# Retention and gated network on one core: idle matmuls, turn order and the third pair's place

## The chip, the core and the metric

The kernel runs on one core of a Trainium2 chip. The metric is the device time of one execution in microseconds. A core has five engines that run their own instruction streams and meet through semaphores: TensorE (PE: matrix products, with weight loads listed as PEld), VectorE (DVE), ScalarE (ACT), GpSimd (POOL) and SyncE (SP, which here issues the DMAs). All times below are microseconds unless another unit is given.

## The reference

```python
def _attn_ref(q, k, v):                      # (8 batches, 8 heads, 576, 64)
    scores = scale * np.matmul(q, k.transpose(0, 1, 3, 2))
    gamma = 1.0 - 2.0 ** (-5.0 - np.arange(H))
    Dmat = np.where(rel >= 0, gamma[:, None, None] ** rel[None, :, :], 0.0)
    return np.matmul(scores * Dmat[None, :, :, :], v)

def _moe_ref(x, w_gate, w_val, w_out):       # x: 4608 x 512; 512 x 1536, 1536 x 512
    gate = 1.0 / (1.0 + np.exp(-(x @ w_gate)))
    return gate * (x @ w_val) @ w_out
```

The heads' outputs of the first function, put side by side, are the rows `x` of the second. There is no softmax; the decay is a power of a number per head, so it can be put into q and k row by row, and what earlier rows contribute can be carried in a state of 64 x 64 per head.

## The kernel before, in words

**Two ways through attention.** Each batch has 576 rows: four chunks of 128 and a short one of 64. Six chunks (batch 0, chunks 0 to 3, and batch 1, chunks 0 and 1) are taken as three *pairs* of 256 rows (`PAIRS`), the other 34 chunks as *steps* (`STEPS`). Every chunk ends as columns of `xT`, the input of the gated network, transposed. 768 columns come from the pairs, the rest follow step by step.

**A pair.** `load_pair` asks for k, q, k, q, v, v (two tiles each, g = 0 and 1, four heads in a tile). `cast_pair` multiplies k (POOL) and q (DVE) by the decay table and narrows v (POOL). `turn` calls `pair_t` (L301): four PE transposes into a PSUM bank and a copy by ACT (L316). `pair_qk` (L318) makes 16 small score products into two banks, and DVE multiplies both by the triangle (L330). `pair_intra` (L356) multiplies these by v, `pair_st` (L333) adds k times v to the state bank, `tile_sv` (L346) copies the state to SBUF in two halves on the engines that it is given (L351), `pair_inter` (L370) adds state times q, and `pair_out` (L378) copies the result to `xT` (L380).

**Idle matmuls.** `fill(n)` (L149) takes a PSUM bank of the `ffn` pool (three banks, shared with the turns of the first two pairs) and runs n products of zeros, 128 rows by 512 columns, whose result nobody reads.

**A step.** `casts_to(s)` (L447) issues for each step up to s: the loads of a following step, POOL's casts of k (L247) and q (L257), the DMA transpose of both (`cross`, L284, on SP), and POOL's cast of v (L268). Then come phases: `phase_qk` (scores, L390, and the mask on DVE, L392), `phase_pv` (L409, L411, and ACT's copy to `xT`, L413) and, in all but short chunks, two `phase_st` (L423, state, with DVE's copies, L429). `order` (L433) lists the phases; `run_phase` (L457) puts `casts_to(s + 3)` ahead of each score phase and ACT's dense copy of the next step's v (`cast_dense`, L278) behind scores and outputs. Buffers for the cast k, q and v go round in fours.

**The order of everything.** The schedule is manual: every engine runs its instructions in the order in which the program lists them. The head is a straight list (L614 to L762): pairs one and two; the gated network's first 512 columns (`h_both`, L592: sigmoid products hg and value products hv for 12 column groups); then the first output products (`op_first`, L720, 12 groups for each of four row blocks) with the third pair between them. After it the loop over `BLOCKS` (L766) runs the network on blocks of 256, 384 and 512 columns, in units of eight products (`h_units`, `op_units`), and between units `advance` runs as many phases as have come due, in proportion to the columns done. `store` copies an output to SBUF, and `tick` issues its DMA on SP some units later. SP thus carries, in one queue and in program order, loads, transposes and stores.

The functions that the diff touches and their callers are printed here with the line numbers of the profile.

Of the kernel before, what the change touches and what calls it, by code (L numbers as in the profile page):

```python
# [9 lines left out]
FP32 = mybir.dt.float32  # L10
# [6 lines left out]
def kernel(  # L17
# [19 lines left out]
    nc = tc.nc  # L37
# [4 lines left out]
    P = 128  # L42
    M = H // 2
    NC = (S + P - 1) // P
# [12 lines left out]
    tr_psum = ctx.enter_context(tc.tile_pool(name="tr_psum", bufs=1, space=PS))  # L57
# [85 lines left out]
    LEAD_CAST = 3  # L143
# [5 lines left out]
    def fill(n):  # L149

        ps = ffn_psum.tile([P, 512], FP32, tag="ffn", name=f"idle_{fill.at}")
        fill.at += 1
        for i in range(n):
            nc.tensor.matmul(ps, lhsT=blank[:, 0:P], rhs=blank, start=True, stop=True)  # L154

    fill.at = 0
    fill(12)
    def tables(shape, pattern, step, put):

        pos = consts.tile([P, pattern[0][1], pattern[1][1]], FP32, name=f"pos{step}")  # L160
# [60 lines left out]
    xT = consts.tile([P, M, NT], BF16)  # L221
# [5 lines left out]
    def cast_pair(nm, A, g, eng):  # L227

        if (nm, A) not in natural:
            natural[nm, A] = osb_pool.tile([P, 2, H, D], BF16, tag="osb", name=f"{nm}p_{A}")  # L230
        o = natural[nm, A][:, :, g * M:(g + 1) * M, :].rearrange("p r h d -> p h r d")
        i = parts.pop((nm, "pair", A, g))
        if nm == "v":
            eng(out=o, in_=i)
        else:
            tab = (ktab2 if nm == "k" else qtab2)[:, PAIRS[A][1], g * M:(g + 1) * M, :].unsqueeze(3).to_broadcast([P, M, 2, D])
            eng.tensor_tensor(out=o, in0=i, in1=tab, op=ALU.mult)
# [33 lines left out]
    def cast_dense(s, j):  # L271

        if s >= NS or STEPS[s][1] == NC - 1:
            return
        if j == 0:
            natural["vs", s] = nat_pool.tile([P, 2, M, D], BF16, tag="vs", name=f"vs_{s}", bufs=2)
        for hh in range(2):
            nc.scalar.copy(out=natural["vs", s][half(hh), j], in_=loaded[s][0][half(j), hh::2, :])  # L278
# [36 lines left out]
            o = turned["qp", A][:, 2 * g:2 * g + 2, :].rearrange("p m (t r) -> p m r t", r=2)  # L315
        eng(out=o, in_=ps)  # L316

    def pair_qk(A, g, psum, tag):  # L318
        ps = [psum.tile([P, 2, 2, P], FP32, tag=tag, name=f"qkp_{A}_{g}_{hh}") for hh in range(2)]
        for i in range(2):  # L320
            m = 2 * g + i
            for r in range(2):
                for a in range(2):
                    for hh in range(2):
                        nc.tensor.matmul(ps[hh][half(a), i, r, :], lhsT=turned["kp", A][half(hh), m, r, half(a)],  # L325
                                         rhs=turned["qp", A][half(hh), m, a * P:(a + 1) * P], start=True, stop=True)
        if g == 0:
            probs["p", A] = att_pool.tile([P, 2, M, 2, P], BF16, tag="ptp", name=f"ptp_{A}", bufs=1)
        for hh in range(2):
            nc.vector.tensor_tensor(out=probs["p", A][:, hh, 2 * g:2 * g + 2], in0=ps[hh],  # L330
                                    in1=trip.unsqueeze(1).to_broadcast([P, 2, 2, P]), op=ALU.mult)
# [14 lines left out]
    def tile_sv(A, a, engs):  # L346
        b, a2 = PAIRS[A]
        c = 2 * a2 + a
        sb = sbd[4 if (b, c) == (0, 3) else (2 * A + a) % 4]
        for hh in range(2):  # L350
            engs[hh](out=sb[half(hh), :, half(hh)], in_=st_tiles[b][half(hh)])  # L351
        state[b, c, 1] = sb
# [3 lines left out]
    def pair_intra(A, g, a):  # L356
        s = 2 * A + a
        if g == 0:
            pair_ps[s] = (tr_psum if a else pv_psum).tile([P, M, P], FP32, tag="tr" if a else "pv", name=f"pvp_{s}")
        ps = pair_ps[s]  # L360
        for i in range(2):
            m = 2 * g + i
            for r in range(2):
                for hh in range(2):
                    nc.tensor.matmul(ps[half(hh), m, :], lhsT=natural["v", A][half(a), r, 2 * m + hh, :],
                                     rhs=probs["p", A][half(a), hh, m, r, :],
                                     start=(m == 0 and r == 0), stop=(m == M - 1 and r == 1),
                                     skip_group_check=True)

    def pair_inter(A, a):  # L370
        b, a2 = PAIRS[A]
        c = 2 * a2 + a
        for m in range(M):
            nc.tensor.matmul(pair_ps[2 * A + a][:, m, :], lhsT=state[b, c - 1, 1][:, m, :],
                             rhs=turned["qp", A][:, m, a * P:(a + 1) * P],
                             start=False, stop=(m == M - 1), skip_group_check=True)

    def pair_out(A, a, eng):  # L378
        t0 = (2 * A + a) * P
        eng(out=xT[:, :, t0:t0 + P], in_=pair_ps[2 * A + a])  # L380

    def phase_qk(s):
        n = width[STEPS[s][1]]
# [50 lines left out]
    for s in range(NS):  # L434
        if STEPS[s][1] < NC - 1:
            order += [("st0", s), ("qk", s), ("st1", s), ("pv", s)]
        else:
            order += [("qk", s), ("pv", s)]

    done = {"ld": 0, "cast": 0}  # L440

# [5 lines left out]
    def casts_to(s):  # L447
        while done["cast"] <= min(NS - 1, s):
            x = done["cast"]
            loads_to(x + (1 if x < 12 else 2))  # L450
            cast_k(x)
            cast_q(x)
            cross(x)
            cast_v(x)
            done["cast"] += 1

    def run_phase(kind, s):  # L457
        if kind == "qk":
            casts_to(s + LEAD_CAST)
            phase_qk(s)  # L460
            cast_dense(s + 1, 0)
        elif kind == "pv":
            phase_pv(s)
            cast_dense(s + 1, 1)
        else:
            phase_st(s, int(kind[2]))
# [52 lines left out]
    def store(opp, r0, hold, eng=None):  # L519

        ob = osb_pool.tile([P, DM], FP32, tag="osb", name=f"ob_{r0}")
        (eng or on_act)(out=ob, in_=opp)  # L522
        stores.append([hold if r0 >= LATE else 10 ** 6, r0, ob])
# [65 lines left out]
    def turn(nm, A, g, pool=ffn_psum, tag="ffn"):  # L589
        pair_t(nm, A, g, pool, tag, on_act)  # L590
# [30 lines left out]
    cast_pair("k", 1, 1, nc.gpsimd)  # L621
    cast_pair("v", 1, 0, on_pool)
    cast_pair("v", 1, 1, on_pool)
    turn("k", 0, 0)
    turn("q", 0, 0)
    fill(1)
    turn("k", 0, 1)
    pair_qk(0, 0, qk_psum, "qk")
    turn("q", 0, 1)
    fill(1)  # L630
    pair_qk(0, 1, qk_psum, "qk")
    pair_intra(0, 0, 0)
    pair_intra(0, 0, 1)
    pair_st(0, 0)
    tile_sv(0, 0, (on_act, on_dve))
    cast_pair("q", 1, 0, nc.vector)
    turn("k", 1, 0)
    pair_intra(0, 1, 0)
    pair_out(0, 0, on_act)
    pair_intra(0, 1, 1)  # L640
    turn("q", 1, 0)
    pair_inter(0, 1)
    pair_out(0, 1, on_dve)
    cast_pair("q", 1, 1, nc.vector)
    pair_st(0, 1)
    fill(1)
    turn("k", 1, 1)
    tile_sv(0, 1, (on_act, on_act))
    pair_qk(1, 0, qk_psum, "qk")
    turn("q", 1, 1)  # L650
    fill(2)
    pair_qk(1, 1, qk_psum, "qk")
    pair_intra(1, 0, 0)
    pair_inter(1, 0)
    pair_intra(1, 0, 1)
    pair_st(1, 0)
    tile_sv(1, 0, (on_act, on_act))
    fill(1)
    pair_intra(1, 1, 0)
    pair_out(1, 0, on_act)  # L660
    pair_intra(1, 1, 1)
    pair_inter(1, 1)
    pair_out(1, 1, on_dve)
    for i in range(2):
        cast_w("g", 0, 2, i, on_pool)
    cast_w("v", 0, 2, 0, on_pool)
# [53 lines left out]
    def op_first(fcs, nbs, opps):  # L720
        for fc in fcs:
            for nb in nbs:
                nc.tensor.matmul(opps[nb], lhsT=gvs[fc][:, nb * P:(nb + 1) * P], rhs=wo_sb[:, fc, :],  # L723
                                 start=(fc == 0), stop=(fc == NFC - 1))

    opps = [ffn_psum.tile([P, 512], FP32, tag="ffn", name=f"op_0_{nb}") for nb in range(3)]
    op_first(range(0, 8), range(3), opps)
    turn("k", 2, 0, tr_psum, "tr")
    turn("q", 2, 0, qk_psum, "qk")
    op_first((8, 9), range(3), opps)  # L730
    turn("k", 2, 1, pv_psum, "pv")
    op_first((10,), range(3), opps)
    turn("q", 2, 1, qk_psum, "qk")
    pair_qk(2, 0, qk_psum, "qk")
    op_first((11,), range(3), opps)
    pair_qk(2, 1, qk_psum, "qk")
    store(opps[0], 0, 1, on_act)
    store(opps[1], P, 2, on_act)
    opps.append(ffn_psum.tile([P, 512], FP32, tag="ffn", name="op_0_3"))
    op_first(range(0, 4), (3,), opps)  # L740
    pair_intra(2, 0, 0)
    pair_intra(2, 0, 1)
    pair_st(2, 0)
    tile_sv(2, 0, (on_act, on_act))
    op_first(range(4, 8), (3,), opps)
    pair_intra(2, 1, 0)
    pair_out(2, 0, on_act)
    pair_intra(2, 1, 1)
    pair_inter(2, 1)
    pair_out(2, 1, on_dve)  # L750
    store(opps[2], 2 * P, 3, on_act)
    op_first(range(8, NFC), (3,), opps)
    pair_st(2, 1)
    tile_sv(2, 1, (on_dve, on_dve))
    store(opps[3], 3 * P, 4, on_act)
    for t in vbd[2:4]:
        nc.gpsimd.memset(t, 0.0)
    for t in qk_nat[2:4]:
        nc.vector.memset(t, 0.0)
    casts_to(1)  # L760
    cast_dense(0, 0)
    cast_dense(0, 1)  # L762

    BLOCKS = [(512, 256), (768, 256)] + [(t, 384) for t in range(1024, 2560, 384)]
    BLOCKS += [(t, 512) for t in range(2560, NT, 512)]
# [45 lines left out]
```

## Time and profile before

| | |
|---|---|
| median of 7 runs | 341.17 (340.77 to 344.43) |
| the profiled execution itself | 342.43 |
| its span, first to last instruction | 340.7 |
| PE busy | 327.1, 96% of the span |
| PEld, DVE, ACT, POOL busy | 186.0, 163.8, 168.0, 185.7 |
| mean granted PE clock | 0.990 |
| DMA over the span | 59.98 MB, 176 GB/s |

The stages on PE in the profiled execution: idle matmuls from 1.25, the first two pairs from 6.34 to 21.70, the network's first 512 columns from 22.57 to 43.9, outputs and the third pair from 43.77 to 59.93, the blocks from there to the end.

How to read it: "PE busy" counts a product from its start to its modelled end, so neighbours overlap and busy is not the same as full speed. A line of the timeline gives start, duration, engine, line of the kernel, operation, what it writes and reads, how many instructions, and in brackets the idle time ahead of it with the instruction that ended it. The clock is a share of full speed. An engine's idle time costs something only if the end of the kernel waits for it.

### The profile page before, as it was taken

To read this page: it belongs to the slowest core of one execution; us is meant where nothing else is said; L and a number is where in the kernel's file an instruction comes from. 1 tells how busy PE (TensorE), PEld (TensorE's weight loads), DVE (VectorE), ACT (ScalarE), POOL (GpSimd) and SP (SyncE) were. 2 spreads that over 40 slices of the span, in tenths; PEclk is the share of its full clock that TensorE was granted. 3 is DMA by queue.
4 is the path that set the end of the run, shared out by engine and by line. 5 is a ranking of instruction groups with operands and counts; after the bars stand their busy time and mean duration, and the time that the engine had idled before them with its cause. 6 is when DMAs were issued, how large, how long until landed. Compare 5 with 4: busy or idle time off the path is not lost.

```text
span 340.7 us, 7321 instructions
## 1 busy us (share of the span) xinstructions
PE 327.1 (96%) x2740; PEld 186.0 (55%) x2774; DVE 163.8 (48%) x328; ACT 168.0 (49%) x344; POOL 185.7 (55%) x327
## 2 busy tenths in 40 slices
PE   7689998999999999999999999999999999999996
PEld 3544444877856556556556655544555455544443
DVE  5644553753845536526536625641674165503320
ACT  6444624745655555445555755354645455323321
POOL 5664588769855889685349975581658400000000
PEclk9789999999999999999999999999999999999999
DMA  7999994899999999999949999992994550020002
GB/s 209 314 374 371 347 224 85 160 201 168 233 224 268 199 193 230 214 240 223 156 124 204 207 202 228 194 175 94 207 226 92 139 63 2 2 92 34 0 31 92
DMA packets 164099, 59.98 MB, mean 176 GB/s; under 512 B 144480, under 2 KB 156000, under 8 KB 164064
## 3 DMA queue, kind: packets, MB, share of 16 engines
q1 hardware_dynamic: 163920, 59.39, 81.6%
q8 instruction: 21, 0.34, 0.5%
q14 instruction: 14, 0.11, 0.1%
q10 hardware_dynamic: 144, 0.13, 0.1%
HBM read 37.75 MB, written 9.44 MB: 138 GB/s over the span
## 4 chain that ended last, share of the span: by engine, by line
PE 91%; DVE 4%; ACT 2%; issue 2%; DVEq 0%
PE h L484 46%; PE op L551 23%; PE hg L600 3%; PE hv L600 3%; PE op L723 3%; PE pv L411 2%; PE pv L409 2%; PE qk L390 2%; PE st L423 2%; PE idle L154 2%; DVE ptp L330 1%; PE op L541 1%; PE qkp L325 1%; ACT qT L316 1%; PE st L340 1%
## 5 line engine op out<-in xcount | busy, mean ns | idle before, releaser
L484 PE MATMUL h<-xT,wg_sb 128*128 128x384 bf16 (+2 forms) x473 | 102.2, 336 | 0.6 <-DVE gv L512 0.2
L484 PE MATMUL h<-xT,wv_sb 128*128 128x384 bf16 (+2 forms) x475 | 102.5, 336 | 0.3
L247 POOL TENSOR_TENSOR qk_nat<-k,ktab 64x256 bf16<-64x256 f32 x120 | 73.3, 611 | 49.6 <-PE st L423 26.8
L512 DVE TENSOR_TENSOR gv<-g,h 128x384 bf16<-128x384 bf16 (+1 forms) x96 | 59.6, 621 | 62.2 <-PE h L484 47.9
L551 PE MATMUL op<-wo_sb,gv 128*128 128x512 bf16 x357 | 84.3, 379 | 0.8
L508 ACT ACTIVATE g<-h 128x384 bf16<-128x384 f32 (+1 forms) x96 | 52.2, 544 | 66.1 <-PE h L484 58.8
L429 DVE CAST sbd<-st 64x256 bf16<-64x256 f32 x104 | 43.7, 420 | 45.6 <-PE st L423 43.3
L484 PEld LDWEIGHTS <-wg_sb 128*128 128x128 bf16 x480 | 43.8, 98 | 31.7 <-issue 0.6
L484 PEld LDWEIGHTS <-wv_sb 128*128 128x128 bf16 x480 | 44.0, 98 | 28.5
L551 PEld LDWEIGHTS <-gv 128*128 128x128 bf16 x372 | 34.2, 98 | 36.3
L268 POOL CAST vbd<-v 64x256 bf16<-64x256 f32 x120 | 47.4, 395 | 11.3 <-PE pv L411 6.8
L278 ACT CAST vs<-v 64x256 bf16<-64x256 f32 x104 | 41.9, 403 | 1.6
L522 ACT COPY ob<-op 128x512 f32<-128x512 f32 x35 | 20.4, 586 | 44.0 <-PE op L551 37.6
L257 POOL TENSOR_TENSOR qk_nat<-q,qtab 128x512 bf16<-128x512 f32 (+1 forms) x34 | 35.4, 1041 | 2.6
L392 DVE TENSOR_TENSOR pt<-qk,tri 128x512 bf16<-128x512 f32 (+1 forms) x34 | 21.3, 625 | 14.6 <-PE qk L390 14.1
L413 ACT CAST xT<-pv 128x512 bf16<-128x512 f32 (+1 forms) x34 | 18.2, 534 | 18.4 <-PE pv L411 18.3
L411 PE MATMUL pv<-pt,vbd 128*128 128x64 bf16 x240 | 18.0, 193 | 0.5 <-DVE pt L392 0.5
L423 PEld LDWEIGHTS <-qk_nat 128*128 128x128 bf16 x208 | 13.1, 98 | 9.1 <-POOL vbd L268 0.4
L409 PE MATMUL pv<-T,sbd 128*128 128x64 bf16 x216 | 17.4, 193 | 0.1
L411 PEld LDWEIGHTS <-vbd 128*128 128x128 bf16 x240 | 15.3, 98 | 3.5
L409 PEld LDWEIGHTS <-sbd 128*128 128x128 bf16 x216 | 15.0, 98 | 3.2 <-issue 0.7
L500 DVE TENSOR_TENSOR gv<-g,h 128x256 bf16<-128x256 bf16 x24 | 9.8, 420 | 11.9 <-ACT g L498 11.5
(73 smaller groups left out, 233.2 us busy)
## 6 DMA issues: line engine op xcount, KB each, us to landing
out_dram<-ob SPq DMA_DIRECT2D x34, 256.0 KB, 2.5
v<-in_v_dram SPq DMA_DIRECT2D x26, 256.0 KB, 4.1
k<-in_k_dram SPq DMA_DIRECT2D x26, 256.0 KB, 4.4
q<-in_q_dram SPq DMA_DIRECT2D x26, 256.0 KB, 5.2
wg<-in_moe_w_gate_dram SPq DMA_DIRECT2D x12, 256.0 KB, 5.8
wv<-in_moe_w_val_dram SPq DMA_DIRECT2D x12, 256.0 KB, 5.6
wo<-in_moe_w_out_dram SPq DMA_DIRECT2D x12, 256.0 KB, 5.3
k32p<-in_k_dram SPq DMA_DIRECT2D x6, 256.0 KB, 5.4
```

Of the source, the lines that this page charges most:

```text
L247: nc.gpsimd.tensor_tensor(out=kn[half(hh), j, :, half(hh)], in0=k32[half(j), hh::2, :], in1=ktab[half(j), c, hh::2].unsqueeze(2).to_broadc ...
L257: nc.gpsimd.tensor_tensor(out=qs[0:n], in0=q32[0:n], in1=qtab[0:n, c, :].unsqueeze(2).to_broadcast([n, H, D]), op=ALU.mult)
L268: nc.gpsimd.tensor_copy(out=vb[half(hh), j, :, half(hh)], in_=v32[half(j), hh::2, :])
L278: nc.scalar.copy(out=natural["vs", s][half(hh), j], in_=loaded[s][0][half(j), hh::2, :])
L392: nc.vector.tensor_tensor(out=pt[:, :, 0:n].rearrange("p m (j t) -> p m j t", t=64), in0=qkp[:, :, 0:n].rearrange("p m (j t) -> p m j t", ...
L409: nc.tensor.matmul(pvp[:, m, half(j)], lhsT=before[:, m, :], rhs=qT[:, m, half(j)], start=True, stop=False)
L411: nc.tensor.matmul(pvp[:, m, half(j)], lhsT=vb[:, j, m, :], rhs=pt[:, m, half(j)], start=before is None, stop=True)
L429: nc.vector.tensor_copy(out=sb[half(hh), :, half(hh)], in_=st_tiles[b][half(hh)])
L484: nc.tensor.matmul(out, lhsT=w_sb[:, kc, fc * P:(fc + 1) * P], rhs=xT[:, kc, t0 + a:t0 + e], start=(kc == 0), stop=(kc == NKC - 1))
L508: nc.scalar.activation(out=g[:, 0:n], in_=h1[:, 0:n], func=AF.Sigmoid)
L512: nc.vector.tensor_tensor(out=gvs[some[0]][:, a:e], in0=g[:, 0:n], in1=h2[:, 0:n], op=ALU.mult)
L551: nc.tensor.matmul(opp, lhsT=gvs[fc][:, nb * P:(nb + 1) * P], rhs=wo_sb[:, fc, :], start=(fc == 0), stop=(fc == NFC - 1))
```

## The change

- **Idle matmuls**: the opening run has 10 in place of 12, and the first two pairs have 18 in eight places in place of 6 in five; 28 in place of 18 in all.
- **Turns back to back**: the second pair's turns follow each other with less between them; its second q cast is issued right behind the first on DVE; the copies of the first states go to ACT in both halves; `pair_out(1, 1)` is split between DVE and ACT.
- **Third pair**: its turns come after one round of output products each, not after eight; scores, state and inside products stand between further rounds; its second scores go to two other PSUM banks; ACT's dense copies for step 0 move ahead of the last rounds; the first output's copy goes to DVE, a half state copy to ACT.
- **Short chunks**: their score phase changes places with the phase ahead of it (the output phase of the step before); `casts_to` for them goes with the output phase.

```diff
-    fill(12)
+    fill(10)
...
-    def pair_qk(A, g, psum, tag):
-        ps = [psum.tile([P, 2, 2, P], FP32, tag=tag, name=f"qkp_{A}_{g}_{hh}") for hh in range(2)]
+    def pair_qk(A, g, banks):
+        ps = [psum.tile([P, 2, 2, P], FP32, tag=tag, name=f"qkp_{A}_{g}_{hh}") for hh, (psum, tag) in enumerate(banks)]
...
-        eng(out=xT[:, :, t0:t0 + P], in_=pair_ps[2 * A + a])
+        if eng is not None:
+            eng(out=xT[:, :, t0:t0 + P], in_=pair_ps[2 * A + a])
+            return
+        for g, half_eng in enumerate((on_dve, on_act)):
+            half_eng(out=xT[:, 2 * g:2 * g + 2, t0:t0 + P], in_=pair_ps[2 * A + a][:, 2 * g:2 * g + 2])
...
-            order += [("qk", s), ("pv", s)]
+            order[-1:] = [("qk", s), order[-1], ("pv", s)]
...
+        short = STEPS[s][1] == NC - 1
+        if kind == ("pv" if short else "qk"):
+            casts_to(s + LEAD_CAST)
         if kind == "qk":
-            casts_to(s + LEAD_CAST)
...
+    QK = [(qk_psum, "qk"), (qk_psum, "qk")]
     turn("k", 0, 0)
     turn("q", 0, 0)
-    fill(1)
+    fill(4)
     turn("k", 0, 1)
-    pair_qk(0, 0, qk_psum, "qk")
+    pair_qk(0, 0, QK)
     turn("q", 0, 1)
-    fill(1)
-    pair_qk(0, 1, qk_psum, "qk")
+    fill(3)
+    pair_qk(0, 1, QK)
     pair_intra(0, 0, 0)
     pair_intra(0, 0, 1)
     pair_st(0, 0)
-    tile_sv(0, 0, (on_act, on_dve))
+    tile_sv(0, 0, (on_act, on_act))
     cast_pair("q", 1, 0, nc.vector)
+    cast_pair("q", 1, 1, nc.vector)
+    fill(2)
     turn("k", 1, 0)
     pair_intra(0, 1, 0)
+    pair_intra(0, 1, 1)
+    fill(2)
+    pair_inter(0, 1)
+    turn("q", 1, 0)
     pair_out(0, 0, on_act)
-    pair_intra(0, 1, 1)
-    turn("q", 1, 0)
-    pair_inter(0, 1)
-    pair_out(0, 1, on_dve)
-    cast_pair("q", 1, 1, nc.vector)
     pair_st(0, 1)
     fill(1)
     turn("k", 1, 1)
+    pair_out(0, 1, on_dve)
+    turn("q", 1, 1)
+    pair_qk(1, 0, QK)
     tile_sv(0, 1, (on_act, on_act))
-    pair_qk(1, 0, qk_psum, "qk")
-    turn("q", 1, 1)
-    fill(2)
-    pair_qk(1, 1, qk_psum, "qk")
+    fill(3)
+    pair_qk(1, 1, QK)
+    fill(1)
     pair_intra(1, 0, 0)
...
-    fill(1)
+    fill(2)
     pair_intra(1, 1, 0)
...
-    pair_out(1, 1, on_dve)
+    pair_out(1, 1, None)
...
-    op_first(range(0, 8), range(3), opps)
+    op_first((0,), range(3), opps)
     turn("k", 2, 0, tr_psum, "tr")
+    op_first((1,), range(3), opps)
     turn("q", 2, 0, qk_psum, "qk")
-    op_first((8, 9), range(3), opps)
+    op_first((2,), range(3), opps)
     turn("k", 2, 1, pv_psum, "pv")
-    op_first((10,), range(3), opps)
     turn("q", 2, 1, qk_psum, "qk")
-    pair_qk(2, 0, qk_psum, "qk")
-    op_first((11,), range(3), opps)
-    pair_qk(2, 1, qk_psum, "qk")
-    store(opps[0], 0, 1, on_act)
-    store(opps[1], P, 2, on_act)
+    op_first((3, 4), range(3), opps)
+    pair_qk(2, 0, QK)
+    op_first((5, 6), range(3), opps)
+    pair_qk(2, 1, [(tr_psum, "tr"), (pv_psum, "pv")])
+    op_first((7,), range(3), opps)
+    pair_st(2, 0)
+    tile_sv(2, 0, (on_act, on_act))
+    cast_dense(0, 0)
+    cast_dense(0, 1)
+    op_first((8, 9, 10, 11), range(3), opps)
+    pair_intra(2, 0, 0)
+    pair_intra(2, 0, 1)
+    pair_intra(2, 1, 0)
+    pair_out(2, 0, on_act)
+    store(opps[0], 0, 1, on_dve)
     opps.append(ffn_psum.tile([P, 512], FP32, tag="ffn", name="op_0_3"))
     op_first(range(0, 4), (3,), opps)
-    pair_intra(2, 0, 0)
-    pair_intra(2, 0, 1)
-    pair_st(2, 0)
-    tile_sv(2, 0, (on_act, on_act))
-    op_first(range(4, 8), (3,), opps)
-    pair_intra(2, 1, 0)
-    pair_out(2, 0, on_act)
     pair_intra(2, 1, 1)
     pair_inter(2, 1)
     pair_out(2, 1, on_dve)
+    store(opps[1], P, 2, on_act)
+    op_first(range(4, 8), (3,), opps)
+    pair_st(2, 1)
+    tile_sv(2, 1, (on_dve, on_act))
     store(opps[2], 2 * P, 3, on_act)
     op_first(range(8, NFC), (3,), opps)
-    pair_st(2, 1)
-    tile_sv(2, 1, (on_dve, on_dve))
     store(opps[3], 3 * P, 4, on_act)
...
-    cast_dense(0, 0)
-    cast_dense(0, 1)
```

## The prediction

> **What bounds the kernel now.** I read the page's slices first, then the clock by stretches, PE's waits, and then the queues that feed PE (POOL, SP, transposes), because PE is busy 96% of the span.
>
> Slices of the page (tenths; PE busy, granted clock):
> ```profile
> PE   7689998999999999999999999999999999999996
> PEclk9789999999999999999999999999999999999999
> ```
> PE is short only in the first ten slices (85 us), and the clock is short only in slices 1 and 2. From about 62 us on PE hardly waits. So the change can only save in the head, and what it saves there stays saved only if the work behind can start earlier too.
>
> The same view by stretches (length, then busy us of PE, PEld, DVE, ACT, POOL, then clock, DMA share, GB/s):
> ```profile
> 9.91:13.32 3.41, 1.89 (x67) 1.37 (x66) 2.85 (x5) 1.51 (x3) 2.08 (x2) 1.00 1.21 293
> 13.32:16.74 3.42, 2.85 (x46) 2.29 (x48) 1.47 (x4) 1.31 (x3) 2.59 (x4) 0.50 1.10 342
> 16.74:20.16 3.42, 3.31 (x58) 2.16 (x57) 2.57 (x4) 1.37 (x4) 2.28 (x5) 0.50 1.09 355
> 6.50:9.91 3.41, 2.33 (x36) 1.49 (x34) 2.00 (x3) 2.50 (x4) 2.26 (x3) 1.00 1.19 299
> ```
> The clock is halved from 13.32 to 20.16, after a stretch in which PE was busy 1.89 of 3.41 us; a stretch with 2.33 kept it. DMA is saturated meanwhile (share over 1).
>
> PE's longest waits (total, times, longest):
> ```profile
> PE qTp L306 <- DVE qp L237: 1.3, 1, 1.3
> PE qkp L325 <- ACT qT L316: 1.3, 2, 0.6
> PE pv L411 <- DVE pt L392: 0.5, 2, 0.2
> ```
> The first is at 13.55, the second at 9.69 and 53.34 (pairs one and three), the third is two short chunks, 0.24 each.
>
> What comes behind: POOL's timeline (start, duration), SP's, and PE's score products:
> ```profile
> 41.85 1.04 POOL L237 TENSOR_TENSOR kp<-k32p,ktab 128x512 bf16<-128x512 f32 x1 [0.27 <-DMA k32p<-in_k_dram]
> 43.61 1.04 POOL L237 TENSOR_TENSOR kp<-k32p,ktab 128x512 bf16<-128x512 f32 x1 [0.72 <-DMA k32p<-in_k_dram]
> 54.13 1.04 POOL L257 TENSOR_TENSOR qk_nat<-q,qtab 128x512 bf16<-128x512 f32 x1
> ```
> ```profile
> 55.20 1.54 SPq L284 DMA_TRANSPOSE T<-qk_nat  x1
> 108.71 2.62 SPq L284 DMA_TRANSPOSE T<-qk_nat  x1
> ```
> ```profile
> 62.12 0.40 PE L390 MATMUL qk<-T 128*128 128x64 bf16 x8
> 115.78 0.40 PE L390 MATMUL qk<-T 128*128 128x64 bf16 x8
> ```
> Transposes' time to landing, asked for at 55.20 and at 108.71:
> ```profile
> T<-qk_nat SPq DMA_TRANSPOSE x1, 4.3
> ```
> ```profile
> T<-qk_nat SPq DMA_TRANSPOSE x1, 4.7
> ```
> The third pair's k arrives by DMA at 41.8 and 43.6. POOL then works without a gap to 55.17, SP asks for step 0's transpose at 55.20, and it lands at 59.5; PE uses it at 62.12, a slack of 2.6. Step 9's lands at 113.4 and is used at 115.78, slack 2.4. I take it that neither time depends on PE: up to 55 the chain is DMA and POOL, and from there to 109 POOL waits five times, 0.4 to 2.3, each ending some 4.3 after SP asked for that step's k (the last is put down to an h product, but its k was asked for at 97.25 and it ends at 101.60), and SP issues without long gaps at DMA shares of 0.7 to 1.3. These slacks cap whatever PE gains.
>
> **The change, part by part.**
>
> *Pairs one and two.* Ten idle matmuls more (28 for 18), 0.216 each at full clock (8 of the 512-column h products take 1.73), 2.2 us. Replayed by hand with the trace's durations: four lie before the k turn that waits for POOL until 7.53, three before ACT's qT (9.3), the rest behind turns that wait for ACT and DVE. They are free as long as those waits last; without cover they cost the 2.2. Two fewer cold ones (0.43) at the start gain nothing: the second k cast (POOL, 7.53) ends that wait.
> The state copy (0,0) goes wholly to ACT (two of 0.37, done at 11.34; DVE's half ended at 12.19). DVE can start pair two's q product at 11.40, before POOL's k product of 11.91. In before it started at 12.22 beside that one and took 1.28; the others took 0.68 to 0.80. So it ends near 12.1, not 13.50. The second q product then ends near 13.55, both k turns follow POOL (12.95), and the chain is: ACT kT 0.59, qT 0.74, xT 0.59, kT, qT (to 15.4), second scores 15.6 (18.20 before), two masks 1.29 to 17.4 (20.17), state copies to 17.8 (21.26), inter product 0.4, and xT(1,1) in two halves on DVE and ACT, 0.4 instead of 0.70. First weight product: 18.9 instead of 22.57, 3.7 earlier. This has the clock at full; some 3.9 us of PE pieces on the chain were at half clock, and if it falls again I estimate half of that, 1.9, back, leaving 1.8. With the idle matmuls 9.9 to 13.3 is nearly full, so I take full.
>
> *Weights.* 96 products of 0.216 and the state product take PE to 40.05; casts are ahead of them (the last value weights of columns 4 to 7 land near 27.4, needed from 29.7). Nothing is lost, but the k of pair three is not cast before 42.89. One round of outputs (0.65, and 0.4 for a bank) ends near 41.1: **a new wait of 1.8 us**, where before had eight rounds first.
>
> *Pair three.* PE work from there: 45 output products 9.7, turns 0.88, scores 0.5, inside products 0.5, states 0.5, inter 0.22: 12.3. The second q cast holds its turn 0.4, the fourth output waits 0.1 for DVE's copy of the first, and 0.1 goes in small gaps. 42.94 + 12.9 = 55.8 for the first h of block 512, instead of 59.93. Before took 16.16 from its first output for 13.0 of work; the 3.2 of waits are what spreading removes. The four dense copies (1.66 on ACT) move ahead, covered by output products.
>
> *What is late next.* PE wants step 0's scores 1.87 after the first h: 57.7. They land at 59.5. Gain at that point: 62.12 - 59.55 = 2.6, **whatever the two parts gained beyond it**. Either part alone would reach nearly the same.
>
> *Short chunks one phase sooner.* The two waits of 0.24 go: 0.5. The six later short chunks had none. Casts stay behind, now one phase after their scores; POOL's order in the built program is unchanged, and on SP one output store moves behind step 8's loads, ACT's and DVE's pieces by one unit. I take nothing for these. At most 0.4 is lost (ACT's dense copy for step 4 may now wait for its load ahead of a sigmoid), and as little may be won, since masks come a unit earlier. Scores of steps 2 to 8 still find their transposes, by 0.5 or more (step 5: landing 86.5, wanted 87.1). Step 9 wants them at 115.78 - 3.05 = 112.7 and gets them at 113.45: gain 2.33, and later slacks are 5 and more.
>
> *The clock.* The Trainium skill (TensorE: Matmul & The Clock Gate, Why this matters for your kernels) warns only of idle gaps over about 3 us. By that rule the waits of 1.8 at 41 and at 57.7 cost nothing. But by it before's clock would not have fallen either: its longest wait there was 1.34. By the row, 1.5 us of idleness in a 3.41 stretch suffices (1.89 busy fell; 20.16 to 23.57, with 2.02, kept), and both new waits can do it. One lost stretch is 1.7 us of PE work. At 41 it would only use up the wait at 57.7 (55.8 + 1.7 = 57.5, scores wanted 59.4): free. At 57.7 it leaves 3.05 - 1.7 = 1.35. I let the row count for the range and take none.
>
> **Sum.** Span 340.70 - 2.33 = 338.37. The profiled execution itself took 342.43, 1.73 more than its span, and would take 340.10. It lies 1.26 above the median of the seven; from the median, 341.17 - 2.33 = 338.84.
>
> **Rivals.**
> - *Likeliest, 338.8, chance 0.45* (338.2 to 339.4): capped by the transposes.
> - *The feed moves along, 0.20*: loads or POOL run earlier too, and the cap lifts to what PE alone gains, 59.93 - 55.8 + 0.5 = 4.6. For: buffers come free earlier. Against: DMA saturated, POOL's order the same. Half the way from 2.33 to 4.6: 337.7.
> - *One clock stretch lost at step 0's wait, 0.22*: 341.17 - 1.35 = 339.8.
> - *It doesn't do what it says, 0.07*: idle matmuls fail to hold the clock, and the freed waits come back in front of pair three's loads: 341.2.
> - *Slower, 0.06*: the wait at 57.7 halves the clock, and it stays so for three stretches (before: two), 3 x 1.71 = 5.1 against 3.05 saved: 343.2. It decides from 1.8 stretches on; against it, PE is full right behind, and a full stretch (3.31) restored it at 20.16.
>
> **Numbers.** 0.5% is 1.7 us, about what a measurement of this kernel can tell from no change: faster below 339.5, slower above 342.9. Faster: 0.42 + 0.20 + 0.06 = 0.68; slower 0.07; same 0.25. The range 337.0 to 340.6 takes in the lifted cap and one lost stretch.
>
> **What would show it.** Clock 1.00 from 6.5 to 20; first weight product near 19; PE waiting about 1.8 for POOL's k near 42.9; first h near 56; PE waiting for T at 57.7 to 59.5, and under 1 us at step 9; no wait for pt in the short chunks. Wrong if PE finds T ready at step 0 (the feed moved), or if the clock row shows a half-speed stretch after 40.

## The result and the profile after

The changed kernel takes 339.56 (median of 22 runs, 338.12 to 342.36), the kernel before, run beside it, 341.65 (57 runs). The ratio is 0.9934, 95% interval 0.9919 to 0.9949: by it 2.25 are saved, against 2.33 forecast (the medians themselves differ by 2.09). The profiled execution of after took 340.89 with a span of 339.2, so in the two profiled executions the difference is only 1.5. Why single executions differ by as much as the gain itself, the experiments showed in part; the rest stays open.

The page's slices of after, the rows shown of before:

```profile
PE   8899999999999899899999999999999999999996
PEclk9999999999999999999999999999999999999999
```

The two short slices of the clock are gone, and PE is short only in its first two slices, a little in slices 14 (110 to 119) and 17 (136 to 144), and in the last. At the head of PE's waits (total, times, longest) now stands one that was not there:

```profile
PE qk L394 <- DMA T<-qk_nat: 2.1, 2, 1.1
PE idle L154 <- DVE blank L147: 1.3, 1, 1.3
PE kTp L306 <- POOL kp L237: 1.0, 2, 0.7
PE hg L606 <- DVE xT L384: 0.6, 1, 0.6
```

The long wait for `qp` (1.3) has shrunk to 0.2, those for `pt` (0.5) are gone; in their place step scores wait for a DMA transpose. PE's timeline has the places (start, duration, idle time ahead in brackets): the first weight product, the k turn of the third pair, and the scores of steps 0, 9 and 13. First before's line for the first of them, then after's:

```profile
22.57 1.02 PE L600 MATMUL hg<-xT,wg_sb 128*128 128x512 bf16 x4 [0.88 <-DVE xT L380]
```
```profile
19.58 1.02 PE L606 MATMUL hg<-xT,wg_sb 128*128 128x512 bf16 x4 [0.61 <-DVE xT L384]
...
42.88 0.40 PE L306 MATMUL kTp<-ident,kp 128*128 128x128 bf16 x4 [0.71 <-POOL kp L237]
...
58.96 0.41 PE L394 MATMUL qk<-T 128*128 128x64 bf16 x8
...
112.75 0.41 PE L394 MATMUL qk<-T 128*128 128x64 bf16 x8 [0.99 <-DMA T<-qk_nat]
...
142.35 0.29 PE L394 MATMUL qk<-T 128*128 128x64 bf16 x4 [1.06 <-DMA T<-qk_nat]
```

And SP's timeline, the transposes of steps 0, 9 and 13:

```profile
55.15 1.54 SPq L284 DMA_TRANSPOSE T<-qk_nat  x1
...
107.81 2.88 SPq L284 DMA_TRANSPOSE T<-qk_nat  x1
...
137.95 2.01 SPq L284 DMA_TRANSPOSE T<-qk_nat  x1
```

PE is 3.0 ahead at the first weight product, but SP asks for step 0's transpose 0.05 sooner than before, for step 9's 0.9 sooner and for step 13's 0.9 later (137.04 in before). The feed did not move along with PE.

How far PE is ahead of before at the same product is the clearest view of where time comes and goes. These are starts read from the PE timelines of the profiled executions, before minus each kernel; only the first column is a start itself, 22.57 in before (blocks are named by their first column and start at 59.93, 96.98, 123.38, 149.55 and 306.12 in before; step 9's scores lie between the second and the third, step 13's about the fourth):

| run | first weight product | h of block 512 | block 1024 | block 1408 | block 1792 | last block |
|---|---|---|---|---|---|---|
| after | 19.58 | 2.86 | 4.18 | 3.01 | 1.43 | 1.55 |
| pairs one and two alone | 20.08 | 2.49 | 2.50 | 2.49 | 2.49 | 2.49 |
| third pair alone | 22.10 | 1.61 | 2.22 | 2.21 | 2.21 | 2.21 |
| short chunks alone | 22.24 | -1.20 | -0.44 | -0.45 | -0.79 | -0.67 |
| after, 18 idle matmuls | 19.02 | 2.78 | 4.04 | 3.66 | 2.39 | 2.51 |
| after, loads two ahead | 19.51 | 3.16 | 3.02 | 2.64 | 2.30 | 2.42 |
| before, loads two ahead | 22.84 | -0.27 | -0.26 | -0.27 | -0.27 | -0.27 |
| after, two short chunks sooner | 19.31 | 3.28 | 4.48 | 4.27 | 4.27 | 4.27 |
| before, 28 idle matmuls | 20.80 | 1.78 | 1.79 | 1.78 | 1.78 | 1.79 |
| order of pairs one and two alone | 19.41 | 3.16 | 3.16 | 2.32 | 2.32 | 2.32 |
| two short, loads two ahead from step 7 | 19.39 | 3.22 | 4.44 | -1.39 | -1.39 | -1.38 |
| the same, 18 idle matmuls | 19.04 | 3.23 | 4.39 | -3.73 | -3.73 | -3.73 |

One run is not in the table: the profiled execution of the changed kernel without the short chunks' part ran in a slower state of the chip (clock 0.95 from beginning to end), so its profile is not used, and its ratio rests on the other five executions.

After wins 3.0 in the first two pairs, nothing more in the third (2.86), 0.4 in block 512 and 0.87 from the short chunks, is 4.18 ahead at 93, and gives back 1.17 at step 9 and 1.46 about step 13 (3.01 to 1.55). The profiled execution of before had two stretches at half clock; how much of each lead is only that comes out below.

### The profile page after: what moved, and what is told of

The parts are those of the page before. It is cut to its first block, busy times and chain, and to the rows that moved or that the text cites. A ratio compares the mean times of both kernels' runs of the same rounds, so it can differ in the third digit from the quotient of the medians.

```text
span 339.2 us, 7347 instructions
## 1 busy us (share of the span) xinstructions
PE 327.3 (96%) x2749; PEld 184.2 (54%) x2784; DVE 163.2 (48%) x327; ACT 168.3 (50%) x346; POOL 185.6 (55%) x327
## 4 chain that ended last, share of the span: by engine, by line
PE 80%; DMA 13%; SPq 3%; issue 1%; DVE 1%; ACT 1%; POOL 0%
PE h L490 46%; PE op L557 22%; DMA wv<-in_moe_w_val_dram 5%; DMA T<-qk_nat 3%; PE op L733 3%; PE qk L394 2%; SPq L114 2%; PE pv L415 2%; DMA q32p<-in_q_dram 2%; PE pv L413 2%; PE st L427 2%; DMA v32p<-in_v_dram 2%; DMA wo<-in_moe_w_out_dram 2%; SPq L105 1%; PE op L547 1%
## 5 line engine op out<-in xcount | busy, mean ns | idle before, releaser
L394 PEld LDWEIGHTS <-T 128*128 128x128 bf16 x240 | 11.4, 98 | 8.2 <-DMA T<-qk_nat 3.0
```

## The experiments

My theory was that the feed (loads, POOL's casts, SP's transposes) caps what PE keeps. The rivals: the parts simply add, or the clock is all of it. Each run is compared with the kernel before on the same chip.

### The parts one by one

Pairs one and two as changed, the rest as before:

```diff
-    fill(12)
+    fill(10)
...
-    tile_sv(0, 0, (on_act, on_dve))
+    tile_sv(0, 0, (on_act, on_act))
     cast_pair("q", 1, 0, nc.vector)
+    cast_pair("q", 1, 1, nc.vector)
+    fill(2)
...
-    pair_out(1, 1, on_dve)
+    pair_out(1, 1, None)
```

> Only the first two pairs are changed (idle matmuls, turns, split copies); third pair and short chunks as before. Theory (the feed caps: what PE wins is kept only up to where the transposes of steps 0 and 9 land): first weight product near 19.6 as in the changed kernel, first h near 57, scores of step 0 held to about 59.0, scores of step 9 within 0.6 of their transpose; 2.6 saved, ratio 0.9925. Rival (the parts add up to the 2.25 that the whole change saved, so each has a share): 1.2 saved at most, ratio 0.9965 or above.

Measured: 339.72, ratio 0.9949 (0.9923 to 0.9974), clock 0.998 or more in all ten runs. The interval takes in both the theory and the rival. In its profile step 9's scores start at 113.28 without a wait.

The third pair's list as changed, the rest as before:

```diff
-    op_first(range(0, 8), range(3), opps)
+    op_first((0,), range(3), opps)
     turn("k", 2, 0, tr_psum, "tr")
+    op_first((1,), range(3), opps)
     turn("q", 2, 0, qk_psum, "qk")
...
```

> Only the third pair is spread over the output products; pairs one and two and short chunks as before. Theory (feed caps): clock still halved from about 13 to 20 and first weight product near 22.6, but no wait for POOL's k; first h at 57.8, scores of step 0 near 59.7; 2.3 saved, ratio 0.993. Rival (parts add): 0.3 to 0.8 saved, ratio 0.998 or above.

Measured: 340.05, ratio 0.9953 (0.9939 to 0.9967): between the two expectations, and outside both. The clock falls as in before (0.990 or 0.995 in 13 of 16 runs).

Only the order of the short chunks' scores, with `run_phase`, as changed:

```diff
-            order += [("qk", s), ("pv", s)]
+            order[-1:] = [("qk", s), order[-1], ("pv", s)]
```

> Only the short chunks' scores come one phase sooner. Theory: the two waits for the mask go, 0.4 each as the products behind them are counted, and no transpose is late, since step 13's is wanted 6.3 sooner out of a slack of 8: 0.8 saved, ratio 0.9976. Rival (the sooner scores cost as much as they save, as step 13's wait of 1.06 in the changed kernel suggests): 0 saved or up to 0.5 lost, ratio 1.000 to 1.0015.

Measured: 341.52, ratio 0.9991 (0.9977 to 1.0006): not told from no change, while the theory's 0.9976 lies just outside the interval. The timeline agrees with the theory as far as it goes: between blocks 512 and 1024 this execution wins 0.76 on before, and there is no wait for a transpose. It is 1.2 late at the first h, because its clock was low longer (0.985 over the span).

The changed kernel with the short chunks as before:

```diff
-            order[-1:] = [("qk", s), order[-1], ("pv", s)]
+            order += [("qk", s), ("pv", s)]
```

> The changed kernel with the short chunks' scores in their old place. Theory: step 13's wait for its transpose (1.06) goes, step 9's shrinks to about 0.5, the two waits for the mask come back; the cap decides, so 2.6 saved against before, as much as the changed kernel or 0.5 more; ratio 0.991 to 0.9935. Rival (parts add, short chunks worth 0.8): 1.45 saved, ratio 0.9958.

Measured: 339.32 (339.07 without the execution that was profiled), ratio 0.9929 (0.9907 to 0.9951). As the theory has it, nothing is seen to be lost without the short chunks' part.

Taken alone, the three parts save 1.7, 1.6 and 0.3, together 3.6 by these ratios, and the whole saves 2.25. The parts do not add; by the intervals the difference of 1.4 is only just clear of noise. Each of the first two wins less than the theory had it (2.6 and 2.3). In their profiles neither is capped: 2.49 and 2.21 stay to the end with no wait for a transpose. A cap can show only in a kernel that is further ahead than that, and one of the next runs is.

### Idle matmuls or the order of the turns

The changed kernel with as many idle matmuls as before (the eight places of the first two pairs get 1, 1, 0, 0, 1, 2, 0, 1 for 4, 3, 2, 2, 1, 3, 1, 2):

```diff
-    fill(10)
+    fill(12)
...
     turn("q", 0, 0)
-    fill(4)
+    fill(1)
     turn("k", 0, 1)
     pair_qk(0, 0, QK)
     turn("q", 0, 1)
-    fill(3)
+    fill(1)
...
```

> The changed kernel with 18 idle matmuls, placed as the kernel before has them (12 at the start; 1, 1, 1, 2, 1), in place of 28; all else as changed. Theory (they hold the clock, but the feed caps what that is worth): a stretch at half clock between 10 and 20, first weight product at 20.6 to 21.6 (19.6 in the changed kernel), less waiting for POOL's k near 42 and for step 9's transpose; 1.2 to 1.9 saved in all, ratio 0.9945 to 0.9965. Rival A (the order of the turns does it, idle matmuls do nothing): clock at 1.00, 19.6, ratio 0.9934. Rival B (the clock is all of it): ratio 0.999.

Measured: 339.36, ratio 0.9938 (0.9913 to 0.9962); clock 0.998 or more in four of six runs, 0.995 and 0.990 in the others. In the profiled execution it never fell. By stretches (length, busy PE, PEld, DVE, ACT, POOL, clock, DMA share, GB/s), and its first weight product in PE's timeline:

```profile
6.50:9.91 3.41, 1.65 (x37) 1.11 (x40) 2.02 (x3) 1.69 (x3) 2.23 (x3) 1.00 1.19 298
9.91:13.32 3.41, 2.74 (x95) 2.30 (x88) 2.46 (x4) 2.05 (x5) 2.18 (x2) 1.00 1.21 292
```
```profile
19.02 1.02 PE L606 MATMUL hg<-xT,wg_sb 128*128 128x512 bf16 x4 [0.61 <-POOL wv_sb L214]
```

With ten idle matmuls less the weight products start 0.56 sooner in these two profiles. Two more pairs of runs below that differ in this alone give 0.67 (20.08 and 19.41) and 0.35 (19.39 and 19.04). So the idle matmuls are not free, as the prediction had them. Here it wins nothing: PE then waits 1.36 for POOL's k at 42.97, and the first h starts no sooner (57.15 against 57.07). The stretch with 1.65 of 3.41 kept its clock: less than the 1.89 after which before's fell. By time it fits rival A (0.9934). The next two runs part the causes further.

The kernel before with 28 idle matmuls in its own waits (10; 4, 3, 2, 4, 1, 2, 2), nothing else changed:

```diff
-    fill(12)
+    fill(10)
...
+    fill(2)
     turn("k", 1, 0)
...
+    fill(4)
     turn("q", 1, 0)
...
```

> The kernel before with 28 idle matmuls instead of 18, put into its own waits in the first two pairs (10 at the start; 4, 3, 2, 4, 1, 2, 2); nothing else changed. Theory (the gain of the first two pairs is the clock, and idle matmuls are what holds it): clock 0.998 or more in every run; the kernel before took 339.65 and 340.05 in its two runs with that clock, against 341.2 at 0.995 and 342.05 at 0.99, so about 339.9, ratio 0.995. Rival (the order of the turns holds the clock): clock still 0.99 to 0.995 in most runs, ratio 0.998 or above.

Measured: 340.32, ratio 0.9968 (0.9955 to 0.9981); clock 0.998 or more in all 22 runs. So the clock is as the theory has it, and the saving, 1.1, is less than its 1.7. First weight product:

```profile
20.80 1.02 PE L600 MATMUL hg<-xT,wg_sb 128*128 128x512 bf16 x4 [0.88 <-DVE xT L380]
```

The changed order of pairs one and two with before's 18 idle matmuls (the first run of this chapter, less its idle matmuls):

```diff
-    fill(10)
+    fill(12)
...
     tile_sv(0, 0, (on_act, on_act))
     cast_pair("q", 1, 0, nc.vector)
     cast_pair("q", 1, 1, nc.vector)
-    fill(2)
     turn("k", 1, 0)
...
```

> The first two pairs in the changed order with split copies, but with the 18 idle matmuls of the kernel before in its places (12; 1, 1, 1, 2, 1); third pair and short chunks as before. Theory (idle matmuls hold the clock): it falls in some runs, 0.990 to 0.995, and ratio lies between 0.996 and 0.998. Rival (order holds it): clock 0.998 or more in nearly all runs, ratio 0.994 to 0.995.

Measured: 339.14, ratio 0.9936 (0.9913 to 0.9959); clock 0.998 or more in seven of eight runs, 0.995 in one. First weight product:

```profile
19.41 1.02 PE L604 MATMUL hg<-xT,wg_sb 128*128 128x512 bf16 x4 [0.61 <-DVE xT L384]
```

This profile also shows the cap without the third pair and the short chunks. PE comes to step 9's scores 3.16 ahead, waits for the transpose, and is 2.32 ahead from there to the end; the prediction puts the cap at step 9 at 2.33:

```profile
113.44 0.41 PE L394 MATMUL qk<-T 128*128 128x64 bf16 x8 [0.67 <-DMA T<-qk_nat]
```

Both rivals hold in part: idle matmuls alone keep the clock, and the order alone nearly keeps it and wins more. Order alone cannot be told from the whole change. My theory that the changed kernel needs its idle matmuls to hold the clock fell.

The granted clock of every single run says what the clock is worth. The runs of the kernel before that stand beside these experiments, 90 of 91 (the slowest, 344.76 at 0.980, is left out), fall into classes:

| clock over the span | runs | median |
|---|---|---|
| 0.998 to 1.000 | 6 | 339.94 |
| 0.993 to 0.995 | 40 | 341.19 |
| 0.989 to 0.990 | 40 | 341.98 |
| under 0.987 | 4 | 343.89 |

One stretch of 3.4 at half clock (as in before's profile, 13.32 to 16.74) is 0.005 of the span's clock. A run of before with two of them (as its profile) takes 2.0 more than one with none, and all 22 runs of after have 0.998 or more. So of the 2.09 between the medians, 1.7 (341.65 - 339.94) is what before's clock costs it in the median, and only 0.4 (339.94 - 339.56) is left for everything else, though after is 4.2 ahead at 93. Six runs stand behind the 339.94, and the 0.4 cannot be told from nothing. In the table of leads, too, about 2.0 of the lead of a kernel that keeps its clock is the clock that before's profile lost.

Sorted so, the first two experiments come apart. Pairs one and two alone took 339.72, always at full clock: next to 339.94 nearly all that it saves is the clock. The third pair alone saves at the same clock: 340.26 against 341.98 in its seven runs at 0.990, 339.66 against 341.19 in its six at 0.995. Together they leave 0.4 at full clock, so by these medians most of what the third pair wins alone is lost in the whole. And the kernel before with 28 idle matmuls, 340.32 at full clock, is about 0.4 slower than with 18, at the edge of the noise: they hold the clock and cost something.

### Where the rest went

The changed kernel with only steps 2 and 3 sooner:

```diff
+        if STEPS[s][1] == NC - 1 and STEPS[s][0] >= 2:
+            order += [("qk", s), ("pv", s)]
-        short = STEPS[s][1] == NC - 1
+        short = STEPS[s][1] == NC - 1 and STEPS[s][0] < 2
```

> The changed kernel, with the sooner scores for the first two short chunks only (steps 2 and 3); the six of the later batches as before. Theory: step 13's wait for its transpose (1.06) goes, since its scores come 6.3 later again; step 9's stays; the gain grows by 1.0 to 1.5: ratio 0.990. Rival (the late transpose only delays a product that would wait elsewhere): ratio 0.9934.

Measured: 339.24, ratio 0.9930 (0.9907 to 0.9953). The profiled execution took 338.16 with a span of 336.4: no wait for any transpose, and 4.27 ahead to the end. The other five runs took 338.29 to 339.92, three of them 339.76 or more; by the median it is the rival's 0.9934 and the theory's 0.990 is missed. Step 13's wait is gone as the theory says. Step 9's is gone too, which the theory did not expect, and that comes at least for the most part from the execution: up to there SP's queue holds the same transfers in the same order as in after, but step 9's transpose was asked for at 106.41, 1.4 sooner, and 0.9 of it was there at step 8's (97.32 against 98.20), the first step that the edit touches.

The changed kernel with loads two steps ahead throughout:

```diff
-            loads_to(x + (1 if x < 12 else 2))
+            loads_to(x + 2)
```

> The changed kernel with the loads of the steps two steps ahead of POOL's casts from the first step on (before: one step ahead up to step 11, then two). Theory (what caps the gain is that loads for steps 7 to 13 come late through SP's queue): POOL's waits for k between 60 and 125 shrink, the waits for the transposes of steps 9 and 13 (0.99 and 1.06) go, the 4.2 that PE is ahead at 93 is kept: ratio 0.988. Rival (POOL's casts or the transposes themselves are the limit, or DMA is full there): the waits stay, ratio 0.993 to 0.994.

Measured: 339.86, ratio 0.9955 (0.9939 to 0.9971): a miss. The waits at steps 9 and 13 shrank to 0.2 and nothing, but step 2's scores now waited 1.16, since SP has to issue step 4's loads ahead of step 2's transpose. The lead of 3.16 fell to 2.14 there. Later transposes did come sooner (step 13's was asked for at 133.92, after's at 137.95).

The kernel before with the same edit:

> The kernel before, with the loads two steps ahead from the first step on. Theory: transposes come sooner, but before has no wait for them, so nothing is gained: ratio 0.9985 to 1.0015. Rival (earlier loads are worth something of their own): 0.997 or less.

Measured: 341.90, ratio 1.0004 (0.9984 to 1.0025): earlier loads are worth nothing where nobody waits for them.

Both ideas joined, with the switch to two steps ahead at step 7:

```diff
-            loads_to(x + (1 if x < 12 else 2))
+            loads_to(x + (1 if x < 7 else 2))
```

> The changed kernel with the sooner scores for steps 2 and 3 only and with loads two steps ahead from step 7's casts on (before: from step 12 on). Theory (late transposes of steps 9 and 13 take back what PE wins): no wait for a transpose over 0.3, the 4.2 to 4.5 of the best single execution is kept every time: ratio 0.989, narrow spread. Rival (what is lost is lost elsewhere): 0.993 as the changed kernel.

Measured: 343.86, ratio 1.0080 (1.0051 to 1.0110): slower than before, against both expectations. SP's and PE's timelines for step 9, and then the clock by stretches:

```profile
110.98 2.85 SPq L284 DMA_TRANSPOSE T<-qk_nat  x1
```
```profile
115.83 0.61 PE L394 MATMUL qk<-T 128*128 128x64 bf16 x8 [3.88 <-DMA T<-qk_nat]
```
```profile
110.50:112.50 2.00, 1.40 (x7) 0.52 (x6) 1.37 (x3) 1.23 (x3) 0.34 (x1) 1.00 1.29 259
112.50:114.00 1.50, 0.00 (x0) 0.00 (x0) 0.00 (x0) 0.00 (x0) 0.47 (x1) 1.00 1.35 218
114.00:115.83 1.83, 0.00 (x0) 0.00 (x1) 0.00 (x0) 0.00 (x0) 1.64 (x4) 0.82 1.03 217
115.83:118.00 2.17, 2.17 (x13) 1.07 (x14) 0.69 (x1) 0.00 (x0) 2.03 (x4) 0.50 1.28 254
118.00:120.00 2.00, 2.00 (x13) 0.94 (x12) 0.53 (x2) 0.59 (x1) 1.76 (x5) 0.86 1.97 155
```

Three more loads stand in SP's queue ahead of step 7's transpose, and with DMA full they push the next transposes back: step 9's is asked for at 110.98 instead of 107.81. POOL is not the cause: it begins step 9's k 3.2 sooner than in after. POOL's timelines, after's and then this run's:

```profile
101.45 2.63 POOL L247 TENSOR_TENSOR qk_nat<-k,ktab 64x256 bf16<-64x256 f32 x4 [3.27 <-DMA k<-in_k_dram]
```
```profile
98.24 2.63 POOL L247 TENSOR_TENSOR qk_nat<-k,ktab 64x256 bf16<-64x256 f32 x4
```

PE waits 3.88, the clock falls near the end of that wait and stays down for one stretch, and the lead goes from 3.99 just ahead of it to -1.39. It is the slower rival of the prediction, in another place and with one stretch instead of three.

The same with 18 idle matmuls, put as above:

```diff
-    fill(10)
+    fill(12)
...
```

> The same as the run before it in this list (two short chunks, loads two ahead from step 7), with the 18 idle matmuls of the kernel before in place of 28. Theory (in the new order 10 idle matmuls cost PE 0.56 ahead of the first weight product, 19.02 against 19.58, and save the clock in some runs only; the wait for POOL's k near 42 hides the difference): within 0.3 of its twin where the clock stays, 0.5 to 1 slower where it falls; ratio 0.989 to 0.991. Rival (idle matmuls are a net cost): 0.5 faster, ratio 0.9875.

Measured: 345.08, ratio 1.0101 (1.0067 to 1.0136). The wait at step 9 is 3.78, step 8 waits 1.52; the trace can say nothing of idle matmuls past that. Both expectations are missed, and on the idle matmuls it is inconclusive.

No run here beats the changed kernel beyond the intervals.

## Why the prediction came out right, step by step

**The total** was right, 2.33 against 2.25, and the mechanism, a gain capped by the transposes of the steps, is there in the profiles (after, and the order of pairs one and two alone). That the numbers agree so closely is in part luck. The sum was worked out on two profiled executions, where PE ends 1.55 ahead and not 2.33; several terms were off and partly cancelled; and the 339.56 itself lies just above the likeliest 338.2 to 339.4, since before, too, took 0.5 more here than in its first seven runs. That either part alone "would reach nearly the same" holds in the profiles (2.49 and 2.21) and less by the medians (1.7 and 1.6). The prediction's own sign of being wrong, that PE finds T ready at step 0, came true, though the feed had not moved (0.05); the cap held at steps 9 and 13 in its place.

- *Pairs one and two*: forecast 18.9, measured 19.58. The step that failed is that the ten idle matmuls are "free as long as those waits last": with 18 in place of 28 it is 19.02. (The three pairs of profiles give 0.35 to 0.67.) Some of them stand past the wait that should hide them. The chain without them was near: 19.02 to 19.41 in three profiles.
- *The wait for POOL's k*: forecast 1.8, measured 0.71 (the 0.42 for a bank ahead of it was foreseen); PE came later, so it waited less, up to the same instant (42.88 against 42.94).
- *The third pair*: forecast 12.9 from there to the first h, measured 14.2. The 12.3 of work was too small: counting products at their spacing within a run leaves out the gap at each change between output products and pair products. In after 24 inside products take 0.56 from their start to the next product of another kind and 8 take 0.34, so some 0.2 is not their number's; 14.2 less 45 output products of 0.216 leaves 4.5 for the pair's products, gaps and waits, where 3.2 were forecast. Forecast 55.8, measured 57.07. In after the spread third pair wins nothing (3.0 ahead at the first weight product, 2.86 at the first h); alone it wins 1.1 up to the first h and 0.6 behind it. The new wait took the place of the old ones.
- *Step 0*: I had the transpose land at 59.5, which would hold PE. It was used at 58.96 without a wait; its time to landing was 3.8, not 4.3, so it came just in time for a PE that was itself 1.3 later than forecast. The first cap did not bind, and PE was 3.2 ahead, not 2.6. (POOL does not work "without a gap" ahead of it in before: at 45.37 it had waited 0.72 for v.)
- *Short chunks*: forecast 0.5, measured 0.87. The waits of 0.24 are counted from the modelled end of the product ahead; what PE loses is start to start, 0.41 each (79.92 to 80.36 in before, where neighbours follow at 0.03).
- *Step 9*: forecast landing at 113.45 and a wait of 0.7; measured 112.75 and 0.99. Right in place and near in size, though PE was 4.2 ahead there in place of 3.05 and the transpose landed 0.7 sooner.
- *Step 13*: not seen. "Later slacks are 5 and more" holds for the old places, but the edit itself moves this score about 6 sooner, besides PE's lead, and its transpose was asked for 0.9 later. I carried the move through for steps 2 to 8 only. The wait costs about the second half of what is lost, and it goes when that score is left in place. In before PE comes to it here:

```profile
150.20 0.28 PE L390 MATMUL qk<-T 128*128 128x64 bf16 x4
```

- *The clock*: I weighed the Trainium skill (TensorE: Matmul & The Clock Gate, Why this matters for your kernels), whose row on drops in mid-kernel warns of gaps over about 3 us, against before's row and let the row widen the range. No new wait of after's profile (up to 1.06) let the clock fall, which fits both readings. That a busy share of about half a stretch decides did not stand: 1.65 of 3.41 kept the clock in one run. The stretches were drawn on before's own change points, and in the run with the third pair alone the clock averages 0.87 from 9.91 to 13.32, so it falls near 12.4, not 13.3: a grid from one execution does not fit another. The 3.88 of the run with loads ahead fits the page: PE stood wholly idle, and the clock fell about 3.2 after its last product. What exactly lets the clock fall in before, with no wait over 1.34, stays open.
- *The rival "the clock is all of it"* had no chance of its own in the prediction; it came up with the experiments, and it is near the truth by size: 1.7 of the 2.09. At full clock before and after differ by 0.4. In the profiles this is so because what PE wins beyond it is given back at the transposes; the execution without those waits kept 4.27.

What stays open is how often steps 9 and 13 wait in executions that were not profiled. That this makes the spread of after's 22 runs (4.2 from fastest to slowest, all at full clock, where before with 28 idle matmuls spreads over 1.2) is argued from two profiled executions, of after and of the kernel with two short chunks sooner, that differ by 2.7 in time and by just these waits; it is not shown for the rest. So the cap is shown in profiles, and its share of the medians is argued.

## What to carry to other kernels

When PE is the bound and a change brings it forward, list the latest times of everything that it reads later, with the edit's own moves put in: the smallest slack on the slowest queue is the gain to count on. In the profiled execution two transposes took back over half of a lead of 4.2. Before filling waits with idle matmuls, try the order: here the reordered turns kept the clock in seven of eight runs, and ten idle matmuls more delayed the next stage by 0.35 to 0.67. Look at the granted clock of every run, not only of the profiled one, before splitting a gain into causes.

## What the runs showed of the hardware

- The same program draws its clock anew in each execution: by their mean clock, before's runs had none, one, two or more half-clock stretches of 3.4 in 6, 40, 40 and 4 of 90 runs, and the medians go from 339.94 to 343.89.
- With DMA full the place in SP's queue decides when a transpose comes: where the loads begin to run one step further ahead, the next transposes come later (step 9's was asked for at 110.98 in place of 107.81, the wait 3.88 in place of 0.99), although POOL began its work for it sooner (98.24 in place of 101.45). Where that step lies far back, they come sooner (step 13's at 133.92 in place of 137.95).
- A wait of 3.88 with PE wholly idle cost 5.4 in all: the clock fell near its end, about 3.2 after PE's last product, and stayed at half for one stretch of 3.4.
- Products of zeros hold the clock: before with ten more of them had 0.998 or more in 22 of 22 runs, without them in 6 of 90.
